# Three score tiles per exp instruction, with a new PE schedule, in a fused attention and MLP kernel

## The chip, the cores and the metric

One core of one Trainium2 chip. The metric is the device time of one execution in microseconds; the span is the time from the first to the last instruction of a profiled execution, here some 1.8 us shorter. Engines: PE (matmul), ACT (ScalarE), DVE (VectorE), POOL (GpSimd), SP (the DMA issuer). The granted clock is the share of its full speed at which PE ran, read from the trace; the row PEclk has it in tenths for 40 slices of the span. A row of a page reads: line of the kernel, engine, operation, output<-input, shapes, count | busy us, mean ns of one | us that the engine stood idle before them, and what ended most of it. Differences of 0.3% are the noise of a run; all medians below are of several executions, and kernels were timed in turn with the kernel before on the same chip.

## The reference

A block with two branches on one layernorm, S = 2048, D = 640, 32 heads of width 20 that share one K and one V, F = 1536, bf16:

```python
xn = layernorm(x)
q = (xn @ wq).reshape(B, S, 32, 20).transpose(0, 2, 1, 3)
k, v = xn @ wk, xn @ wv
p = softmax(einsum("bhqd,bkd->bhqk", q, k) * 20**-0.5)
attn = einsum("bhqk,bkd->bhqd", p, v).transpose(0, 2, 1, 3).reshape(B, S, 640) @ wo
h = relu(xn @ w1 + b1) ** 2
return x + attn + h @ w2 + b2
```

The scores alone are 32 x 2048 x 2048 exponentials: 2048 tiles of 128 keys by 512 queries (one head), 512 columns each.

## The kernel before

The kernel records every operation into one queue per engine, with the semaphore waits that its reads and writes need, and then emits the queues. After a prologue of some 40 us (layernorm, transposes, K, V) it runs 32 blocks (a group of four heads by 512 queries). A unit is four score tiles, one key chunk for the four heads: PE fills four PSUM banks with scores, ACT takes exp of two banks at a time into SBUF, PE multiplies by V into the accumulator bank (PV). All else, the FFN, the output projection, the next block's Q, is cut into pieces and put into the slots of these units on PE, DVE and POOL.

```python
def pe_fill(u):                       # four row-tiled matmuls, one for each head of the group
    for r in range(4):
        h = 2 * u + r // 2
        bk = (h % 3) * 2 + (r % 2)    # three pairs of banks
        e.matmul(bank(bk), lhsT=KT_aug[32*r:32*r+21, kc*128:(kc+1)*128],
                 rhs=QT[32*r:32*r+21, qs, :], tile_position=(32*r, 0))
def act_exp(h):                       # 1024 columns
    e.activation(out=PT[:, h % 8, :], in_=ps[:, bk*512:bk*512+1024], func=Exp, scale=SCALE)
def pe_pv(u, npad):                   # four column-tiled matmuls; npad dummy matmuls keep PE busy
    ...
# (prologue, DVE and POOL steps cut)
pe_fill(0)
for u in range(NU):                   # NU = 512 units
    act_exp(2 * u)
    if u + 1 < NU: pe_fill(u + 1)
    act_exp(2 * u + 1)
    if u >= 1: pe_pv(u - 1, sl.npad(u))
    run_slot_lists(u)                 # the pieces placed in this slot
```

At a block's end DVE copies the accumulator bank to SBUF (O_un) before the next block's first PV may write it; two sets of transposes and a reciprocal normalise it.

## Time and profile before

| | before |
|---|---|
| median of 15 runs | 996.69 us (994.99 to 997.77) |
| span of the profiled run | 994.8 us |
| exps on ACT | 1024, from 40.24 to 983.65 us |
| period of the exps in an unbroken run | 0.917 us |
| from the last exp's end to the end of the span | 11.2 us |
| granted PE clock, mean | 0.996 |

How to read it: find the engine that the chain follows (ACT), then the period of its instruction rather than its mean duration, then the places where the run of that instruction breaks. The prediction below does this with the lines themselves. One more reading: the record of an exp begins when it is handed to ACT, which may be before the exp ahead of it ends (1024 records of 1.24 us on average cover only 940 us, so they overlap). So its shortest record (1018 ns) is an exp that came to an idle ACT, and the surplus of a record over that is time it stood ready: the lead that PE has. Before, the surplus is at most 1332 − 1018 = 0.31 us.

### The profile page before, as it was taken

The numbers are of one execution on the slowest core, as the hardware profiler recorded it, in microseconds if no ns is written. First come the engines' busy times: TensorE is split into PE (matmuls) and PEld (weight loads), VectorE is DVE, ScalarE is ACT, GpSimd is POOL, SyncE is SP. The second block draws the span as 40 slices with busy tenths as digits, with TensorE's granted clock in tenths as the row PEclk, the third lists the DMA queues.
The fourth block names the chain that finished last, engine by engine and source line by source line (L and its number), as shares of the span: only waits on it lengthen the run. The fifth ranks groups of instructions, "written<-read, shape, count | busy, mean of one in ns | idle before, by whom it ended". The sixth has DMA issues, their size and how long they took to land.

```text
span 994.8 us, 16761 instructions
## 1 busy us (share of the span) xinstructions
PE 829.7 (83%) x7455; PEld 296.3 (30%) x7455; DVE 218.9 (22%) x445; ACT 958.6 (96%) x1059; POOL 110.3 (11%) x144
## 2 busy tenths in 40 slices
PE   3878899878998888899888888987778887788886
PEld 2422344222432322244322223432222222222222
DVE  7422222221221222222221222211011211021212
ACT  5599999999999999999999999999999999999995
POOL 7321100121000012200120010000000000000000
PEclk9999999999999999999999999999999999999998
DMA  9100000000000000000000000000000000000000
GB/s 299 35 1 1 1 1 2 1 1 1 1 2 14 14 1 1 2 1 1 1 1 14 14 1 1 2 1 1 1 1 2 13 14 2 1 1 1 1 1 27
DMA packets 9817, 11.93 MB, mean 12 GB/s; under 512 B 1873, under 2 KB 9074, under 8 KB 9746
## 3 DMA queue, kind: packets, MB, share of 16 engines
q1 hardware_dynamic: 9218, 10.46, 3.3%
q8 instruction: 58, 0.95, 0.4%
q10 hardware_dynamic: 432, 0.25, 0.1%
q0 software_dynamic: 96, 0.16, 0.0%
q14 instruction: 13, 0.11, 0.0%
HBM read 8.25 MB, written 2.62 MB: 11 GB/s over the span
## 4 chain that ended last, share of the span: by engine, by line
ACT 90%; PE 6%; DVE 2%; DMA 1%; SPq 0%; issue 0%; POOL 0%
ACT PT L1119 90%; PE ps L463 2%; PE ps L1135 1%; PE ps L1098 1%; PE ps L1131 1%; DMA wk_raw<-in_A_wk_dram 1%; DVE O_un L1162 1%; PE ps L1169 1%; DVE r_tmp L924 1%; PE ps L1010 0%; SPq L500 0%; PE ps L729 0%; DVE stats L648 0%; DVE out_stage L1333 0%; DVE stats L645 0%
## 5 line engine op out<-in xcount | busy, mean ns | idle before, releaser
L1119 ACT ACTIVATE PT<-ps 128x1024 bf16<-128x1024 f32 x1024 | 940.0, 1240 | 8.9 <-PE ps L1098 8.9
L1098 PE MATMUL ps<-QT,KT_aug 21*128 21x512 bf16 x2048 | 202.3, 385 | 124.5 <-ACT PT L1119 118.8
L1135 PE MATMUL ps<-ones_bf,zeros_bf 128*32 128x512 bf16 x859 | 255.8, 379 | 0.0
L1131 PE MATMUL ps<-PT,V_aug 128*32 128x512 bf16 x2048 | 204.9, 390 | 8.0 <-DVE O_un L1162 7.3
L1098 PEld LDWEIGHTS ps<-QT,KT_aug 21*128 21x128 bf16 x2048 | 52.0, 91 | 315.9 <-ACT PT L1119 298.8
L970 POOL TENSOR_TENSOR Qsq<-QT 128x512 bf16<-128x512 bf16 x32 | 33.2, 1038 | 644.3 <-DVE QT L965 644.2
L1135 PEld LDWEIGHTS ps<-ones_bf,zeros_bf 128*32 128x32 bf16 x859 | 82.8, 96 | 50.9
L1131 PEld LDWEIGHTS ps<-PT,V_aug 128*32 128x32 bf16 x2048 | 52.6, 93 | 125.1 <-issue 108.3
L463 PE MATMUL ps<-xnT,w_sb 128*128 128x512 bf16 x240 | 68.4, 383 | 1.3 <-DVE QT L979 0.2
L931 POOL TENSOR_TENSOR h2T<-r_tmp 128x512 bf16<-128x512 bf16 x48 | 49.9, 1039 | 177.5 <-DVE r_tmp L924 177.5
L924 DVE TENSOR_SCALAR r_tmp<-ps,b_sb 128x512 bf16<-128x512 f32 x48 | 36.0, 751 | 136.4 <-PE ps L463 136.4
L463 PE MATMUL ps<-w_sb,h2T 128*128 128x160 bf16 x768 | 64.2, 234 | 0.0
L463 PEld LDWEIGHTS ps<-w_sb,h2T 128*128 128x128 bf16 x768 | 51.6, 98 | 27.2 <-DVE out_acc L1243 21.7
L1162 DVE COPY O_un<-ps 128x512 f32<-128x512 f32 x32 | 22.0, 688 | 155.2 <-PE ps L1135 134.0
L949 PE MATMUL ps<-xnT,wq_raw 128*20 128x512 bf16 x640 | 51.9, 380 | 0.0
L463 PE MATMUL ps<-wo_pad,OTn 128*128 128x320 bf16 x256 | 48.1, 313 | 0.5 <-DVE OTn L1196 0.5
L1243 DVE TENSOR_TENSOR out_acc<-ps,x_sb 128x160 f32<-128x160 f32 x64 | 20.8, 325 | 103.3 <-PE ps L463 103.3
L965 DVE CAST QT<-ps 128x512 bf16<-128x512 f32 x31 | 21.5, 692 | 95.9 <-PE ps L949 95.9
L979 DVE SCALAR_TENSOR_TENSOR QT<-ps,sc,QT 128x512 bf16<-128x512 f32 x32 | 24.0, 751 | 49.8 <-PE ps L974 49.7
L463 PEld LDWEIGHTS ps<-wo_pad,OTn 128*128 128x128 bf16 x256 | 20.5, 100 | 33.9 <-issue 24.3
L1196 DVE COPY OTn<-ps 128x512 bf16<-128x512 bf16 x32 | 13.6, 425 | 71.8 <-PE ps L1188 71.8
L1333 DVE TENSOR_TENSOR out_stage<-ps,out_acc 128x320 bf16<-128x320 f32 x24 | 11.8, 492 | 73.0 <-PE ps L463 73.0
(114 smaller groups left out, 300.7 us busy)
## 6 DMA issues: line engine op xcount, KB each, us to landing
w_sb<-in_B_w_dram SPq DMA_DIRECT2D x2, 1920.0 KB, 10.7
x_sb<-in_A_x_dram SPq DMA_DIRECT2D x8, 320.0 KB, 5.7
out_dram<-out_stage SPq DMA_DIRECT2D x12, 160.0 KB, 1.8
wq_raw<-in_A_wq_dram SPq DMA_DIRECT2D x1, 800.0 KB, 7.2
wo_pad<-in_A_wo_dram SPq DMA_DIRECT2D x4, 200.0 KB
out_dram<-h2T SPq DMA_DIRECT2D x3, 80.0 KB, 1.6
out_dram<-h2T ACTq DMA_DIRECT2D x3, 80.0 KB, 1.6
out_dram<-h2T POOLq DMA_DIRECT2D x2, 80.0 KB, 2.1
```

The source lines that it names most:

```text
L463: ins = e.matmul(outap, lhsT=l, rhs=r, start=(first and i == 0), stop=(last and i == n - 1))
L924: pl.op("dve", (lambda e, j=j, b=b, s=s: e.tensor_scalar(out=r_tmp[:, s, :], in0=bank(b), scalar1=b1_sb[:, j:j + 1], scalar2=0.0, op0=ALU. ...
L931: pl.op("pool", (lambda e, j=j, c=c, s=s: e.tensor_tensor(out=h2T[:, c % 2, j, :], in0=r_tmp[:, s, :], in1=r_tmp[:, s, :], op=ALU.mult)), ...
L949: ins = e.matmul(ps[32 * r:32 * r + DH, b * 512:(b + 1) * 512], lhsT=wq_raw[:, ft, h * DH:(h + 1) * DH], rhs=xnT[:, ft, qc * 512:(qc + 1) ...
L965: pl.op("dve", (lambda e, s=s, b=b: e.tensor_copy(out=QT[:, s, :], in_=bank(b))), reads=[rB[b]], writes=[rQT[s]], expect={rB[b]: ("qp", bl ...
L970: pl.op("pool", (lambda e, s=s: e.tensor_tensor(out=Qsq[:], in0=QT[:, s, :], in1=QT[:, s, :], op=ALU.mult)), reads=[rQT[s]], writes=[rQSQ] ...
L979: pl.op("dve", (lambda e, s=s, b=b: e.scalar_tensor_tensor(out=QT[:, s, :], in0=bank(b), scalar=scc(C_CVEC), in1=QT[:, s, :], op0=ALU.add, ...
L1098: ins = e.matmul(bank(bk), lhsT=KT_aug[32 * r:32 * r + 21, kc * 128:(kc + 1) * 128], rhs=QT[32 * r:32 * r + 21, qs, :], start=True, stop=True,
L1119: pl.op("act", (lambda e, bk=bk, s=s: e.activation(out=PT[:, s, :], in_=ps[:, bk * 512:bk * 512 + 1024], func=ACT.Exp, scale=SCALE)), read ...
L1131: ins = e.matmul(ps[32 * c:32 * c + 32, ACCB * 512:ACCB * 512 + 512], lhsT=V_aug[:, kc, :], rhs=PT[:, s, (c % 2) * 512:(c % 2) * 512 + 512 ...
L1135: ins = e.matmul(ps[0:32, ACCB * 512:ACCB * 512 + 512], lhsT=zeros_bf[:, 0:32], rhs=ones_bf[:, 0:512], start=False, stop=True, tile_positi ...
L1162: pl.op("dve", lambda e: e.tensor_copy(out=O_un[:], in_=bank(ACCB)), reads=[rB[ACCB]], writes=[rOUN], expect={rB[ACCB]: ("acc", blk, KC - ...
```

## The change

Its intent: fewer and wider exp instructions. Three tiles (1536 columns) per exp need three-bank groups; six banks give two of them. The fill becomes one per exp and every PE piece is cut and placed anew, for slots of 1.3445 us in place of 1.834. FFN1, FFN2, Wo and the block-sum matmul become column-tiled, four matmuls of 32 output partitions each, as PV is.

```diff
+        TPI = 3
+        NI = (NT + TPI - 1) // TPI                 # 683 exps
+        SLOT_US = 0.065 + TPI * 0.4265
+        def pe_fill(i):
+            half = i % 2                           # two groups of three banks
+                for k, t in enumerate(tiles):
+                    u, r, blk, kc = tile_info(t)
+                    ins = e.matmul(bank(TPI * half + k), lhsT=KT_aug[...], rhs=QT[...], ...)
+        def act_exp(i):
+                e.activation(out=PTv[:, sidx, 0:n], in_=ps[:, TPI * half * 512:TPI * half * 512 + n], func=ACT.Exp, ...)
...
+        def mm_group_ct(e, bnk, ncols, pairs, first=True, last=True):
+            for i, (l, r) in enumerate(pairs):
+                for c4 in range(4):
+                    ins = e.matmul(ps[32*c4:32*c4+32, ...], lhsT=l[:, 32*c4:32*c4+32], rhs=r, ..., tile_position=(0, 32*c4))
...
-    HAM_TARGET = 0.86                              # pads until so much of 1.834 us is busy
+    HAM_FRAC = 0.42                                # a share of the slot (before: 0.86 / 1.834 = 0.47)
-        NQ2 = 4
+        NQ2 = 2                                    # FFN2 in 320 columns
...
-        for u in range(NU):
-            act_exp(2 * u) ... pe_fill(u + 1) ... act_exp(2 * u + 1) ... pe_pv(u - 1, npad)
+        pe_fill(0); pe_fill(1)
+        for i in range(NI):
+            act_exp(i)
+            if i + 2 < NI: pe_fill(i + 2)
+            (the PVs whose last tile exp i makes, or pads)
+            run_slot_lists(i)
```

(Indices and the slot bookkeeping are cut.)

## The prediction

> **What bounds the kernel now.** I read the page's engine shares first, then the chain that ended last, then the exp row, then the chain in order of time around one interruption, then the timeline of single PE slots. The page of the kernel before:
>
> ```profile
> PE 829.7 (83%) x7455; PEld 296.3 (30%) x7455; DVE 218.9 (22%) x445; ACT 958.6 (96%) x1059; POOL 110.3 (11%) x144
> ...
> ACT 90%; PE 6%; DVE 2%; DMA 1%; SPq 0%; issue 0%; POOL 0%
> ...
> L1119 ACT ACTIVATE PT<-ps 128x1024 bf16<-128x1024 f32 x1024 | 940.0, 1240 | 8.9 <-PE ps L1098 8.9
> ```
>
> ACT is busy 96% of the span and is 90% of the chain, all of it the 1024 exps of line 1119. The mean of 1240 ns is not what one exp costs: 1024 × 1.24 would be 1270 us, but they cover 940.0, so neighbours overlap. The cost to use is the period. The chain in order of time, same kernel (start us, us, what):
>
> ```profile
> 574.59 0.75 DVE r_tmp L924
> 575.34 0.61 DVE O_un L1162
> 575.95 0.04 issue
> 575.99 0.40 PE ps L1131 x4
> 576.39 0.64 PE ps L1135 x3
> 577.03 0.59 PE ps L1169 x4
> 577.61 0.36 PE ps L1098 x4
> 577.97 0.02 issue
> 577.99 200.90 ACT PT L1119 x219
> ```
>
> 219 exps run for 200.90 us without a break. The source views of the exp and of the 512-wide copy on ACT give the isolated durations (min/median/max ns):
>
> ```profile
> L1119 ACT ACTIVATE PT<-ps x1024: 1018/1280/1332, 40.2 to 982.3; 128x1024 bf16<-128x1024 f32 x171
> ```
>
> ```profile
> L741 ACT ACTIVATE xnT<-ps x8: 592/594/597, 16.5 to 31.6; 128x512 bf16<-128x512 bf16 x8
> ```
>
> Period: (200.90 − 1.02) / 218 = 0.917 us. Slope: (1018 − 592) / 512 = 0.832 ns a column. So 1024 columns are 0.852 us and each exp pays about **0.065 us** that does not depend on its width. The exps run from 40.24 (start in the chain) to about 983.65 (last start 982.3 plus up to 1.33; the PV that waits for it starts at 983.70), 943.4 us. Back to back they would be 1.02 + 1023 × 0.917 = 939.1. So some 4.3 us is interruptions, and the first fence shows what these are: at the end of a block the copy of the accumulator (O_un) queues behind r_tmp on DVE, the in-order PE waits for it, and the next fill is late. Everything else on PE, DVE, POOL is beside the exps. The 8.9 us of idle in the exp row has 5.5 us before the first exp in it (longest single wait in the view of waits).
>
> **What the Trainium skill says.** "ScalarE: Activation LUTs", section "What ACT_TABLE_LOAD costs", gives an ACTIVATE with immediate scale and bias 186 ns + 0.833 ns a column, with back-to-back ones overlapping by about 93: a fixed 93 ns each. The trace agrees on the slope (0.832) but has 65 ns fixed; I use 65. "TensorEngine Tiling (Array Packing)", section "Key Properties", says a change of tiling mode drains TensorE. The trace agrees: below, the row-tiled fill holds PE for 0.32 us before PV can start, while a group in the same mode follows after 0.22. "TensorE: Matmul & The Clock Gate", Part 1, says the clock halves when the PE is too little busy; this is what the pad matmuls of line 1135 are for, and the page's PEclk row is 9 in all slices but the last, which is 8. No page says what 8 PE instructions in the time of one 320-column stream cost.
>
> **The change part by part.** (1) *Exp width.* 1024 exps of 1024 columns become 682 of 1536 and one of 1024 (the built program's ACT order says so). Columns do not change, 341 fixed costs go: 341 × 0.065 = **22.2 us off the path**. The new period is 1536 × 0.832 + 65 = 1.343 us.
>
> (2) *Buffers.* PSUM had three pairs of banks, now two triples. Fill i+2 waits for the end of exp i in both. In the loop of two periods before: 0.05 (exp end to fill) + 0.40 (fill) + 0.05 + 1.018 (isolated exp) = 1.52 of 1.834, slack 0.31 us. After: 0.05 + 0.40 + 0.05 + 1.44 (1.018 + 512 × 0.832) = 1.94 of 2.686, **slack 0.74 us**. So PE may be late by twice as much before ACT notices.
>
> (3) *PE slots.* One fill per exp instead of one per two; each brings a mode change. The costs, from PE's timeline of the kernel before, in two kinds of slot (start us, us):
>
> ```profile
> 422.73 1.00 PE L463 MATMUL ps<-w_sb,h2T 128*128 128x160 bf16 x12
> ...
> 423.57 0.23 PE L463 MATMUL ps<-b_pad,r0sel 128*128 128x160 bf16 x1
> ```
>
> ```profile
> 859.96 0.40 PE L1098 MATMUL ps<-QT,KT_aug 21*128 21x512 bf16 x4 [0.47 <-ACT PT L1119]
> ...
> 860.28 0.40 PE L1131 MATMUL ps<-PT,V_aug 128*32 128x512 bf16 x4
> ...
> 860.51 0.81 PE L1135 MATMUL ps<-ones_bf,zeros_bf 128*32 128x512 bf16 x3
> ```
>
> Starts are what to read; the bracket is PE waiting 0.47 us for an exp. Fill to PV 0.32 (0.216 plus about 0.10 of drain), PV to pad 0.23, pad (0.81 − 0.38) / 2 = 0.215. A four-wide column-tiled group of 512 columns: the Q projection's 12 matmuls show 0.83, less 0.40 for one group, over 2: 0.215, as much as one full matmul. A 160-column matmul (423.57 − 422.73) / 12 = 0.070, so 320 columns are estimated at 0.137. Forward transposes 0.58, backward 0.53 to the next fill. I walked the changed PE order with these (fill, then what stands up to the next fill, plus 0.10 to change back): mean **1.17 us** of 1.343 a slot. 90 of 680 slots exceed 1.343: 31 with forward transposes (1.46), 31 with backward ones (1.61 to 1.62), the rest by 1 ns. Carrying each excess into the next slot, the worst lateness is 0.28 us, under 0.74. So PE stays off the path.
>
> (4) *Column tiling of FFN1, FFN2, Wo.* Keeps PE in PV's mode: one drain fewer where they follow PV. Instructions rise from 7455 to some 9700; pads fall from 862 to 708. FFN2 evictions go from 64 of 160 to 32 of 320 columns. All beside the exps.
>
> (5) *Block ends.* The new slots mostly put the O_un copy in a slot of its own, with r_tmp one or two slots earlier. The copy, released by the last PV and its pads at about 1.0 after the fill, ends at 1.9; the next PV is due at 1.343 + 0.32 = 1.67: PE is late by 0.2 and the transposes add 0.12 to it. Also under 0.74: most of the 4.3 us should go.
>
> (6) *Tail.* One Wo chunk with its 0.49 us add now stands between the last PV and the last O_un copy: estimate +0.9 us. The final Wo matmuls are 64 column-tiled ones in place of 16; the same columns, so no change.
>
> Sum: first exp at 40.24; exps 1.44 + 681 × 1.343 + 0.917 = 917.0, end 957.2. Tail before 994.8 − 983.65 = 11.15, plus 0.9: span 969.3. The timed run was 996.57 against a span of 994.8, so +1.8: 971.1 with no interruption at all. I add 2 us for those I cannot see: **973**.
>
> **Rivals.** *Four times the PE instructions cost more than the columns.* A 320-column group has 4 loads and 4 matmuls in 0.137, 17 ns each; the densest run in the trace is the Q projection, 27 ns each. Were a group to need 0.22, the mean slot would be 1.24, but the FFN2 and Wo slots stand together: the same walk then loses about 11 us, 984. For it: nothing in the trace is so dense. Against: the group starts of PV are a few ns apart. *Double buffering starves ACT*, since two triples look shallower than three pairs: speaks against it that the loop is two exps long in both, and longer in time now; if I have the latency wrong by 0.5 us, each block end and transpose costs, 5 to 15 us. *The clock falls*, as there are fewer pads and a lower target (0.42 of a slot against 0.86 / 1.834 = 0.47): then fill, PV and the rest double, 1.17 becomes over 2 and PE is the bound, over 1100. Against: the counts keep a slot without PV at three pads. *O_un waits stay*: 976. *A three-bank read costs ACT more*: each 10 ns is 7 us.
>
> **Range and chances.** Low end 968: no interruption, fixed cost 60. High end 983: the dense-group rival nearly whole, or 15 ns more an exp. The 2% line is 976.8, only 3.8 us above my number, so a small residue takes it to within 2%. Faster 0.72, within 0.27, slower 0.01.
>
> **What would show it.** The exp row: 682 × 1536, busy near 917, idle after the first exp under 3 us. Long unbroken exp runs in the chain give the period: 1.34 is right, 1.37 is not. PE's waits: fills nearly always end an idle wait on ACT; if PE is continuously busy and ACT waits for the fill, steps 2 to 4 fell. The start-to-start of the FFN2 groups tests 0.137. PEclk must stay 9. I am wrong if ACT idles in FFN2 stretches, if the period holds more than 0.08 of fixed cost, or if the tail grows by several us.

## The result, and the profile after

973.57 us (973.21 to 974.88, 8 runs) against 996.69: the ratio is 0.9771, 95% interval 0.9761 to 0.978. Ratios here are the mean time of one kernel's fast runs over that of the other's of the same rounds, so not quite the ratio of the medians. All eight runs were of the fast state.

The page of the changed kernel, the lines that answer to those of before:

```profile
PE 849.1 (87%) x9717; PEld 289.6 (30%) x9717; DVE 213.2 (22%) x413; ACT 936.7 (96%) x718; POOL 110.4 (11%) x144
...
PEclk9899999999999999999999999999999999999999
...
ACT 91%; PE 5%; POOL 2%; DVE 1%; issue 0%; POOLq 0%; ACTq 0%
...
L1173 ACT ACTIVATE PT<-ps 128x1536 bf16<-128x1536 f32 (+1 forms) x683 | 918.0, 1795 | 6.9 <-PE ps L1146 6.6
```

ACT is as full as before (96%) and just as much the chain; it simply has less to do. PE has more instructions (9717 for 7455) and a larger share, 87%, and is still not in the chain.

The source view of the exp and the chain in order of time give the period and the breaks:

```profile
L1173 ACT ACTIVATE PT<-ps x683: 1445/1792/2191, 39.3 to 957.0; 128x1536 bf16<-128x1536 f32 x171
```

```profile
39.34 1.46 ACT PT L1173
...
48.87 365.56 ACT PT L1173 x272
415.19 0.71 PE ps L482 x20
415.92 0.49 DVE out_acc L1330
416.41 0.61 DVE O_un L1241
...
427.97 244.63 ACT PT L1173 x182
...
686.15 271.54 ACT PT L1173 x202
```

The period is (365.56 − 1.445) / 271 = 1.3436 us, or (271.54 − 1.445) / 201 = 1.3438. The largest surplus of a record is 2191 − 1445 = 0.746 us: the slack, against 0.31 before. After the start the chain leaves ACT in only two stretches (at 415 and 673 us), where before it did in ten.

Where the 23.3 us of span went:

| stretch | before | after | difference |
|---|---|---|---|
| up to the first exp | 40.24 | 39.34 | −0.9 |
| first exp's start to last exp's end | 943.4 | 919.3 | −24.1 |
| last exp's end to the end | 11.2 | 12.9 | +1.7 |

In the middle row, 341 exps fewer at (0.917 − 0.853) = 0.064 us are 21.8; the rest is that breaks of 4.3 us became 1.9 (the exps from the end of the first, 40.80, back to back: 681 x 1.3436 + 0.917 = 915.9 of 917.8). The −0.9 is not the change's: other profiled runs of kernels with the same prologue began their exps at 39.7 to 40.3.

A block's end is worth seeing in both kernels (timeline: start us, us, engine, line, operation). Before, at the break that the prediction shows in the chain:

```profile
575.99 0.40 PE L1131 MATMUL ps<-PT,V_aug 128*32 128x512 bf16 x4 [0.68 <-DVE O_un L1162]
```

PE and DVE at such a place in the changed kernel:

```profile
415.02 0.72 PE L482 MATMUL ps<-w_sb,h2T 128*32 128x320 bf16 x16
...
415.56 0.31 PE L482 MATMUL ps<-b_pad,r0sel 128*32 128x320 bf16 x4
...
415.92 0.49 DVE L1330 TENSOR_TENSOR out_acc<-ps,x_sb 128x320 f32<-128x320 f32 x1 [4.88 <-PE ps L482]
416.33 0.68 DVE L1241 COPY O_un<-ps 128x512 f32<-128x512 f32 x1
...
417.06 0.40 PE L1189 MATMUL ps<-PT,V_aug 128*32 128x512 bf16 x4 [0.86 <-DVE O_un L1241]
```

The queue on DVE is the same as before the change, here with an FFN2 eviction ahead of O_un, and PE stands still 0.86 us, longer than the 0.68 before. But with 0.75 us of lead ACT hardly sees it: the two stretches of the chain that begin in this way, at 415 and 673 us, cost ACT 0.2 us each (by the ends of the exps), almost all of it not at the O_un wait but some 10 us later, where the block-sum matmul of the next Q waits for POOL's square of Q:

```profile
427.20 0.40 PE L482 MATMUL ps<-Qsq,blocksel 128*32 128x512 bf16 x4 [1.03 <-POOL Qsq L990]
```

The fill behind it starts at 427.53, 1.00 us after the end of the exp that frees its banks. The least in this trace is 0.05, so it is 0.95 late, over the lead of 0.75. The longer fence above also tests the estimate of the column-tiled groups: 16 matmuls of 320 columns start within 415.56 − 415.02 = 0.54 us, 0.135 us for four.

### The profile page after: what moved, and what is told of

Same layout as the page of the kernel before. It is cut to its first block, busy times and chain, and to the rows that moved or that the text cites. A ratio compares the mean times of both kernels' runs of the same rounds, so it can differ in the third digit from the quotient of the medians.

```text
span 971.5 us, 20895 instructions
## 1 busy us (share of the span) xinstructions
PE 849.1 (87%) x9717; PEld 289.6 (30%) x9717; DVE 213.2 (22%) x413; ACT 936.7 (96%) x718; POOL 110.4 (11%) x144
## 4 chain that ended last, share of the span: by engine, by line
ACT 91%; PE 5%; POOL 2%; DVE 1%; issue 0%; POOLq 0%; ACTq 0%
ACT PT L1173 91%; PE ps L1146 1%; PE ps L1189 1%; PE ps L482 1%; PE ps L969 1%; PE ps L1030 0%; POOL wo_pad L609 0%; PE ps L474 0%; PE ps L1193 0%; POOL xn_tmp L729 0%; PE ps L749 0%; PE ps L1213 0%; POOL Qsq L990 0%; POOL rstd L710 0%; DVE KT_aug L811 0%
## 5 line engine op out<-in xcount | busy, mean ns | idle before, releaser
L1173 ACT ACTIVATE PT<-ps 128x1536 bf16<-128x1536 f32 (+1 forms) x683 | 918.0, 1795 | 6.9 <-PE ps L1146 6.6
L1146 PE MATMUL ps<-QT,KT_aug 21*128 21x512 bf16 x2048 | 268.0, 386 | 83.4 <-ACT PT L1173 71.1
L1193 PE MATMUL ps<-ones_bf,zeros_bf 128*32 128x512 bf16 x339 | 110.6, 380 | 0.0
L1213 PE MATMUL ps<-ones_bf,zeros_bf 128*32 128x512 bf16 x369 | 104.5, 383 | 5.7 <-DVE O_un L1241 5.7
L482 PE MATMUL ps<-xnT,w_sb 128*32 128x512 bf16 x960 | 81.7, 380 | 0.0
L482 PE MATMUL ps<-w_sb,h2T 128*32 128x320 bf16 x1536 | 73.5, 300 | 0.0
L482 PE MATMUL ps<-wo_pad,OTn 128*32 128x320 bf16 x1024 | 54.1, 305 | 1.5 <-DVE out_acc L1379 1.0
L482 PEld LDWEIGHTS ps<-w_sb,h2T 128*32 128x32 bf16 x1536 | 42.3, 96 | 14.5 <-issue 1.1
L1213 PEld LDWEIGHTS ps<-ones_bf,zeros_bf 128*32 128x32 bf16 x369 | 26.1, 95 | 52.1 <-issue 30.8
L1193 PEld LDWEIGHTS ps<-ones_bf,zeros_bf 128*32 128x32 bf16 x339 | 32.7, 96 | 13.5 <-issue 0.3
L482 PEld LDWEIGHTS ps<-wo_pad,OTn 128*32 128x32 bf16 x1024 | 28.3, 98 | 16.7 <-issue 2.0
L482 PEld LDWEIGHTS ps<-xnT,w_sb 128*32 128x32 bf16 x960 | 26.2, 96 | 18.9 <-DVE r_tmp L944 3.2
```

What stands on the lines that cost most here:

```text
L482: ins = e.matmul(ps[32 * c4:32 * c4 + 32, bnk * 512:bnk * 512 + ncols], lhsT=l[:, 32 * c4:32 * c4 + 32], rhs=r, start=(first and i == 0), ...
L1146: ins = e.matmul(bank(TPI * half + k), lhsT=KT_aug[32 * r:32 * r + 21, kc * 128:(kc + 1) * 128], rhs=QT[32 * r:32 * r + 21, blk % 2, :], s ...
L1173: pl.op("act", (lambda e, half=half, sidx=sidx, n=n: e.activation(out=PTv[:, sidx, 0:n], in_=ps[:, TPI * half * 512:TPI * half * 512 + n], ...
L1193: ins = e.matmul(ps[0:32, ACCB * 512:ACCB * 512 + 512], lhsT=zeros_bf[:, 0:32], rhs=ones_bf[:, 0:512], start=False, stop=True, tile_positi ...
L1213: ins = e.matmul(ps[0:32, ACCB * 512:ACCB * 512 + 512], lhsT=zeros_bf[:, 0:32], rhs=ones_bf[:, 0:512], start=False, stop=True, tile_positi ...
```

## The experiments

**One exp cut in two, everywhere.** All of the change is kept, but each three-bank exp is issued as 512 and 1024 columns.

```diff
-  e.activation(out=PTv[:, sidx, 0:n], in_=ps[:, b0:b0 + n], func=Exp)
+  e.activation(out=PTv[:, sidx, 0:512], in_=ps[:, b0:b0 + 512], func=Exp)
+  e.activation(out=PTv[:, sidx, 512:n], in_=ps[:, b0 + 512:b0 + n], func=Exp)
```

> The changed kernel with each three-bank exp cut into two instructions of 512 and 1024 columns over the same banks; all else, the fill order and the slots, as in the changed kernel. Fixed-cost theory (the gain is 341 exps' fixed cost): 682 fixed costs of 0.063 us come back, period 1.343 + 0.063 = 1.406, so 973.6 + 43 = 1016 us, slower than even the kernel before. Rival (the gain is from the new PE schedule and fewer waits, the exp width is beside the point): within 1% of 973.6, as PE has the same work and more time for it.

(The cuts of the code here and below are shortened.)

Measured 1019.43 us, ratio to the kernel before 1.0226 (1.0209 to 1.0243). Against the changed kernel's 0.9771 that is 45 us for 682 cuts, 0.066 us each. With the fixed cost put back twice over the kernel is slower than before the change; the schedule did not save it.

**As many exps as before.** Only every second exp is cut, which makes 1024 in the new schedule.

```diff
+  if half == 0:
+      return e.activation(out=PTv[:, sidx, 0:n], in_=ps[:, b0:b0 + n], func=Exp)
   (else the two of the experiment above)
```

> The changed kernel with every second three-bank exp cut into 512 and 1024 columns: 1024 exps in all, as many as in the kernel before, in the new schedule with all of its buffers, column tiling and pads. Fixed-cost theory: 341 fixed costs come back, 973.6 + 341 x 0.063 = 995 (and by the 0.067 that each cut cost in the run with all exps cut, 996.5): the gain is gone, the time is that of the kernel before. Rival (the schedule brought part of it): 985 or less.

Measured 994.74 us, ratio 0.9985 (0.9978 to 0.9992). Its chain in order of time, pieces of the uncut exps:

```profile
49.07 1.34 ACT PT L1176
51.82 1.34 ACT PT L1176
```

Two slots take 51.82 − 49.07 = 2.75 us, one uncut exp of 1.344 and a cut pair of 1.406: the cut costs 0.062. With the number of exps of before, the time is that of before: this is the gain, located. The 0.15% that stays is small. In the profiled runs the exps take 940.6 us here and 943.4 before, and the tail 13.3 and 11.2: breaks that went, less a longer tail.

**Two tiles per exp in the new schedule.** The other way to take the width back: TPI = 2.

```diff
-        TPI = 3
+        TPI = 2
```

> The changed kernel with two score tiles per exp in place of three: the new schedule, column tiling and two alternating bank groups, but 1024 exps of 1024 columns. Fixed-cost theory: at best 1024 x 0.917 = 939 us of exps, so 993 or more; and as each exp now needs its own fill and mode change, the PE walk gives a mean slot of 0.94 against a period of 0.917, some 36 us of waits: 1010 to 1035. Rival (the re-slotting gives the gain): about 975.

It took 1058.24, 1100.64, 1120.59 and 1196.94 us: no verdict, as the runs differ in their granted clock (0.998, 0.953, 0.932, 0.856). The page of the slowest:

```profile
PE 1148.3 (96%) x9879; PEld 320.4 (27%) x9879; DVE 213.6 (18%) x413; ACT 1001.4 (84%) x1059; POOL 110.4 (9%) x144
...
PEclk9655599999999999855555556999999999999999
```

PE, at 96%, is the bound, and its clock halves for long stretches. Even the run with the clock up missed my upper figure by 23 us. That is one run, and its trace was not kept: it shows the direction, while the size was beyond my walk, which counted no wait but its own. It speaks for, but does not prove, that a fill for each exp, with its mode changes, is only affordable because the exps are longer.

**The same without pads.** To give PE room, the pads of that kernel were left out.

```diff
-        return max(0, min(k, max(room, 0)))        # number of pads in a slot
+        return 0
```

> Two score tiles per exp in the new schedule, as in the run that took 1058 to 1197, but without its pad matmuls (151 us of PE work). There PE was the bound. Theory: the walk gives a mean slot of 0.68 us against 0.917, with bursts that cost some 19 us against a slack of 0.31, so if the clock holds the time is set by 1024 exps of 0.917 again, 993 to 1015 us: no gain over the kernel before from the new schedule alone. If the clock falls below 0.9: over 1050. Rival (the new schedule by itself gives the gain once PE has room): under 985.

1212.64 us (1202.29 to 1219.2), clock 0.627 in the profiled run. So the case that I hoped for, the clock holding, did not occur; this run says nothing on the schedule alone, and the experiment with 1024 exps has to carry that.

**The changed kernel without pads.** The same edit on the changed kernel.

> The changed kernel without any pad matmul in its slots. Clock theory (the pads are there to keep the granted clock up, and PE's slack is only there at the full clock): the granted clock falls below 0.9; at half clock the mean slot would be 0.89 x 2 = 1.78 us against a period of 1.343, so PE becomes the bound in such stretches: 1050 to 1270 us, changing from run to run. Rival (the real work of the shorter slots keeps the clock up by itself): clock over 0.98 and 973.5 within 2 us.

1028.67 us (1024.54 to 1031.38), ratio 1.0318; granted clock 0.804. The exp row of its page:

```profile
L1173 ACT ACTIVATE PT<-ps 128x1536 bf16<-128x1536 f32 (+1 forms) x683 | 931.0, 1510 | 46.4 <-PE ps L1146 45.2
```

ACT waits 45.2 us for fills where it waited 6.6. It was better than my range by 21 us, as PE was slow for part of the time only, but the clock theory holds: 708 matmuls that compute nothing are worth 55 us.

**Full-array matmuls again.** Column tiling undone for FFN1, FFN2, Wo and the block sum.

```diff
         def mm_group_ct(e, bnk, ncols, pairs, first=True, last=True):
+            return mm_group(e, bank(bnk, ncols), pairs, first, last)
```

> The changed kernel with FFN1, FFN2, Wo and the block-sum matmul as full-array matmuls again (no column tiling), everything else as changed. Slack theory: the mean PE slot grows from 1.15 to 1.19 us by mode changes, still under 1.343 with a lateness never over the slack of 0.74: same, 973.6 within 1 us. Rival (column tiling is what lets PE keep up with the shorter slots): 5 us or more slower, with ACT waiting for fills in the FFN stretches.

974.61 us (972.79 to 975.69), ratio 0.978 (0.9767 to 0.9794): the same as the changed kernel. The column tiling, a good part of the diff, neither gains nor costs; its extra instructions and the drains that it saves both lie beside the exps.

**The fill at the end of the slot.** PE does the same work in another order.

```diff
             act_exp(i)
-            if i + 2 < NI: pe_fill(i + 2)
             (PV, pads, run_slot_lists)
+            if i + 2 < NI: pe_fill(i + 2)
```

> The changed kernel with the fill moved to the end of its PE slot, behind the PV, the pads and the background matmuls, which all take the same time as before. Loop theory (the fill of exp i+2 can start when exp i ends, and has 0.74 us of slack): the mean work ahead of the fill is 0.82 us and in heavy slots 1.1 to 1.3, so the fill comes too late in most; carrying the PE walk through the loop gives 44 us more, 1018. Rival (two triples are ample and PE's mean load of 1.15 in 1.343 is all that matters): unchanged within 3 us.

1028.15 us (1025.69 to 1029.57), ratio 1.0314, 55 us more than the changed kernel. The exp row:

```profile
L1173 ACT ACTIVATE PT<-ps 128x1536 bf16<-128x1536 f32 (+1 forms) x683 | 937.4, 1448 | 39.7 <-PE ps L1146 35.5
```

The mean record is 1448 ns, against 1795: practically every exp now comes to an idle ACT, and the lead is gone. PE's share is lower than before (82% for 87%) and the kernel is slower: what counts here is not how much PE does but how much of it stands ahead of the fill. I had put it at 44 us.

**O_un first, in the kernel before.** One line of the old kernel: the copy goes ahead of whatever stands in its slot on DVE.

```diff
-            sl.add(first_slot, "dve", (lambda blk=blk: fin_evac_acc(blk)), 0.6)
+            sl.dve[first_slot].insert(0, (lambda blk=blk: fin_evac_acc(blk)))
+            sl.dve_us[first_slot] += 0.6
```

> The kernel before with one thing moved: the copy of the accumulator at a block's end stands first in its slot on VectorE, ahead of the FFN1 eviction. Theory (the 0.35 to 0.5 us stops at block ends come from that queue): 9 to 12 stops of 0.35 to 0.5 us vanish, 4 us faster than before, ratio 0.996. Rival (they come from PE's own load at the block end): unchanged within 0.5 us.

992.06 us (991.41 to 992.34), ratio 0.9956 (0.9943 to 0.9968). Its chain in order of time has one piece where the kernel before had many:

```profile
40.15 938.94 ACT PT L1119 x1024
```

(938.94 − 1.02) / 1023 = 0.9168, the bare period over all 1024 exps. The breaks were the DVE queue and nothing else, and were worth 4.4 us; the changed kernel got some of that by its larger slack.

**The tail.** The timeline of DVE at the end of the changed kernel, the last exp having ended at 958.60:

```profile
958.67 0.49 DVE L1379 TENSOR_TENSOR out_acc<-ps,out_acc 128x320 f32<-128x320 f32 x1 [1.87 <-PE ps L482]
...
959.73 0.49 DVE L1379 TENSOR_TENSOR out_acc<-ps,out_acc 128x320 f32<-128x320 f32 x1 [0.56 <-PE ps L482]
...
960.78 0.49 DVE L1379 TENSOR_TENSOR out_acc<-ps,out_acc 128x320 f32<-128x320 f32 x1 [0.56 <-PE ps L482]
961.19 0.68 DVE L1241 COPY O_un<-ps 128x512 f32<-128x512 f32 x1
```

Three Wo chunks with their adds, taking turns on one bank, stand ahead of the last accumulator copy, which starts 2.6 us after the last exp (before the change 984.15 − 983.65 = 0.5). The experiment puts these partial sums in banks that the scores no longer need and lets the final matmuls add to them:

```diff
+  if kind == last_stage and max(es1, sl.misc_free) >= NI - 2:
+      deferred.append((tt, ch)); continue         # not placed in a slot
...
+  for d in deferred[:2]: op_early(*d, bank_for[d], [4, 5])    # start=True, no eviction
   pe_pv(NU - 1, 0)
   fin_evac_acc(NB - 1)
+  for d in deferred[2:]: op_early(*d, bank_for[d], [4, 5])
   ...
-  op_pe(tt, ch, gs=[6, 7], bnk=..., first=True)
+  op_pe(tt, ch, gs=[6, 7], bnk=bank_for[(tt, ch)], first=(tt, ch) not in deferred)
```

> The changed kernel with the three Wo chunks (groups 4 and 5) that its schedule leaves for after the last fill put straight into banks that are free by then, to be finished by the final Wo matmuls: three VectorE adds of 0.49 us and their ping-pong on one bank go from the tail. Theory (the tail grew by 1.7 us because these three stand ahead of the last accumulator copy): the copy starts 0.5 us after the last exp as before the change, in place of 2.6, 2 us less: 971.6. Rival (the tail is set by the final 64 matmuls or the clock there): unchanged within 0.5 us.

970.45 us (970.07 to 971.58), ratio 0.9739 (0.9726 to 0.9753). The copy, in its timeline:

```profile
959.10 0.69 DVE L1241 COPY O_un<-ps 128x512 f32<-128x512 f32 x1 [2.57 <-PE ps L482]
```

The last exp ended at 958.31, so it starts 0.8 us after. That is 1.8 us less; another 1 us came from the final 64 matmuls, which took 2.36 us in this run and 3.43 in the changed kernel, with the clock at 1.00 up to 965 us; in the changed kernel it was 0.86 from 960 to 965. Whether the shorter tail keeps the clock up is not shown.

**The start.** The table of stretches of the changed kernel (us; busy time of PE, PEld, DVE, ACT, POOL; PEclk; DMA share, GB/s):

```profile
40.00:42.00 2.00, 1.15 (x9) 0.38 (x9) 0.00 (x0) 1.91 (x2) 0.00 (x0) 1.00 0.01 3
42.00:44.00 2.00, 1.87 (x19) 0.39 (x15) 0.00 (x0) 2.00 (x3) 0.00 (x0) 0.51 0.00 0
44.00:46.00 2.00, 2.00 (x19) 0.39 (x15) 0.00 (x0) 2.00 (x2) 0.00 (x0) 0.50 0.00 0
```

From 42 to 48.5 us the PE runs at half clock, and two exps start late (ACT waits 0.5 us at 46.93 and 48.87). Before the change the clock was 1.00 there. This is not in every run: the profiled run with full-array matmuls, whose start has the same fills and pads, has a clock of 1.00 from 40 to 50 us and loses no exp time to it, and the one with the mended tail has 0.85, 0.50 and 0.79 from 42 to 48 and loses 0.24 us, where this one loses 1.3 (by the ends of the exps). The edit:

```diff
             pe_fill(1)
+        pe_pads(6)
         for i in range(NI):
```

> The changed kernel with six pad matmuls between the second fill and the third. Theory (PE idles 1.34 us after the second fill, the clock falls to half at 42 us and fills are late until 48.6, costing 1.4 us of exps): the clock stays at 1.0 from 42 to 49 us and the time falls by 1 to 1.5 us: 972.3. Rival (the clock falls [...]whatever six pads do): unchanged within 0.5 us.

973.07 us (973.04 to 973.43), ratio 0.9765 (0.9752 to 0.9778): no gain that can be told from noise, the rival's number. But its mechanism is not the rival's. In the profile the clock is 1.00 from 42 to 49, and the exps take 39.7 to 957.71, 918.0 us for 919.3, as hoped. Then the tail took 13.6 us in place of 12.9:

```profile
961.00:965.00 4.00, 2.38 (x20) 1.46 (x24) 1.37 (x3) 0.00 (x0) 0.00 (x0) 0.52 0.00 0
```

There the clock fell to 0.52, where the changed kernel's was 0.86 from 960 to 965. What was won at the start was lost in the profiled run to a later start of the exps and a slower clock in the tail. And in runs where the clock stays up at the start by itself, there was little to win. How far the place of the fall in the tail is chance, these runs do not show.

**Both, and more of the tail done early.** The pads at the start, the deferred chunks, and group 6 of the final sums issued while PE waits for DVE.

> Both of these, and also group 6 of the final Wo sums done early in the tail, in banks that are free. Theory: the sum, 3.4 us, plus up to 0.5 for the shorter final matmuls: 969.8. Rival: the tail is bound by its eight VectorE adds and the last store, and only the 2 us of the chunks come: 971.5.

970.48 us (969.9 to 970.84), ratio 0.9737 (0.9724 to 0.975): the same as the tail alone. The number lies between the two forecasts (969.8 and 971.5); the mechanism is the rival's, as nothing came on top of the mended tail. The final matmuls take 1.41 us in place of 2.36, but the eight DVE adds behind them take 3.27 us in both: they are the bound of the end, then the last stores. The two versions with the mended tail beat both kernels, by 26 us against before and 3 against the changed one.

## Why the prediction was right or wrong

The time, 973.57 for 973.0, the sign and the mechanism were right. Step by step:

- **Step 1, exp width: right.** The predicted period of 1.343 us was measured as 1.3436. Cutting exps put back 0.062 to 0.066 us each; with 1024 exps the gain was gone. Shown.
- **Step 2, slack: right.** 0.74 predicted, 0.746 read from the longest exp record. That the order of the fill within the slot matters as the loop says was shown by moving it (55 us; 44 had been worked out).
- **Step 3, PE slots: right in the conclusion, one term mis-sized.** The backward transposes were given as 0.53 us to the next fill. That figure contained a wait for an exp, and in the changed kernel the step takes 0.33 us start to start. So a slot with backward transposes is 1.41 us in place of 1.61, and one with forward ones, 1.45, has the largest excess, 0.11; the walk's 0.28 was too much. But the walk had only PE's own work in it: with the waits for DVE and POOL, fills were up to 0.95 us late (step 5). The estimate of 0.137 us for a 320-column group was 0.135. PEclk did not stay at 9 throughout: the second slice is 8, at a cost in exps of about 1.3 us in the profiled run (919.3, and 918.0 in the run with the clock up).
- **Step 4, column tiling beside the exps: right,** shown by undoing it.
- **Step 5, block ends: right in the sum, wrong in the detail.** I said that O_un stands in a slot of its own and PE is late by 0.2 us, and 0.12 more with the transposes. PE waits up to 0.9 us for O_un; the waits did not go, they became affordable, and only just. Counted from the 0.05 us that a fill needs at least after the end of its exp, seven fills behind block ends come 0.77 to 0.78 late, which costs ACT 0.02 to 0.04 us each, and two come 0.95 late behind the wait for POOL's square of Q, which the prediction did not have: 0.2 us each. The breaks fell from 4.3 to 1.9 us, of which about 1.3 is the clock at the start.
- **Step 6, tail: wrong in size.** "One Wo chunk with its 0.49 us add" was three, as the pieces in the slots after the last fills also run after the last exps; the tail grew by 1.7 us and not by 0.9.

The 2 us added "for those I cannot see" and an earlier first exp in the profiled run covered these misses; the closeness of the total is partly luck.

Of the rivals, the one of dense instructions fell (0.135 us for a group). Its premise, that nothing in the trace is so dense, was a misreading: the 20 V projection matmuls at 39.2 us of the kernel before start every 25 ns, each with its weight load, 12 ns an instruction. The rival of a dearer three-bank read fell too (the fixed cost is 0.063 to 0.065 for two banks and three). The one of the clock did not come about in this kernel, but is real: take the pads away and it does.

## What to carry to other kernels

Where one engine is full, price its instruction by the period in an unbroken run, split that by two widths into a part for each column and a fixed part, and count how many fixed parts a wider instruction removes; that number is the gain, and all else has only to stay out of the way. Check what stays out of the way as a loop, from the end of an instruction to the start of the one that reuses its buffer, and not by the busy share of the other engine: the same PE work in another order cost 55 us. Look at what a new schedule leaves over for the end; it runs in series there, and was the cheapest thing left to mend.

## What the Trainium skill lacked or had wrong

- "ScalarE: Activation LUTs", section "What ACT_TABLE_LOAD costs": its 186 ns less 93 ns of overlap would leave 93 ns for each ACTIVATE in a row. These runs show 0.064 us at 1024 columns and 1.3436 − 1536 x 0.000833 = 0.064 at 1536, with its 0.833 ns a column; cutting an exp cost 0.062 to 0.066. The passage does not say in which memory its tile lay, and these exps read PSUM and write SBUF, so it may be another case rather than an error.
- "TensorEngine Tiling (Array Packing)", section "Key Properties", names the drain at a change of mode without its price: about 0.10 us here (0.32 against 0.22 to the next start).
- "TensorE: Matmul & The Clock Gate", Part 1, does not say how much dummy work is enough. Here 708 pad matmuls of 512 columns, one to three in 368 of 681 slots of 1.34 us, kept a mean clock of 0.994; without them it was 0.804, and the time 55 us longer, though PE never stood idle for more than 1.3 us while the exps ran.
- No page has the time from one column-tiled group of four to the next, with its weight loads, at 320 columns: 0.135 us, the same as from one full-array matmul of 320 columns to the next (Wo, in the kernel before).
